# A fused attention and spectral-mix kernel: two more units of the output stage take the last mode's rows by a table, unit 3 goes in halves, and one weight tile is issued ahead of a gate

## The chip, the cores and the metric

One core of a Trainium2 chip runs the whole kernel. The metric is device microseconds (us) of one execution; a kernel's time is the median of its runs. The span is the part of one profiled execution from its first to its last recorded instruction; the profiled execution also has a time of its own, which is a little longer than its span.

## The reference

Two parts are computed one after the other; shapes are batch 8, 8 heads, 576 tokens, head size 64.

```python
# attention: window of 128 keys, a linear distance penalty per head
scores = q @ k.T / sqrt(64); scores = where(0 <= rel < 128, scores - slope[h] * |rel|, -1e9)
x = softmax(scores) @ v                 # [8, 576, 512] after joining the heads
# spectral mix: 64 complex modes, each with a 512 x 512 weight w_r + i w_i (float32, 1 MB each)
X = rfft(x, axis=tokens)[:, :64]
Y = X @ (w_r + i w_i)                   # mode by mode
u = x + irfft(Y)                        # the other modes are zero
out = u + relu(u @ w_ch)                # w_ch is 512 x 512
```

The weights of the 64 modes are 128 tiles of 1 MB in float32, which the DMA casts to bfloat16 (512 KB) as it loads them.

## The kernel before, in words

The order on each engine is the program's own order (a manual schedule); waits are semaphores set by a tile library that tracks which part of which tile is read and written.

**Attention** runs over 16 units (a batch and a group of four heads) in the order of the list `STAGE`. The q, k and v of a unit are loaded by the SP queue (lines L211, L215, L222) into the raw buffers, two units deep. Between the stages GpSimd (POOL) issues weight tiles (`load_w`, L462), one per stage into the pool `early`. A one-element copy on POOL (L556), called the gate, ties each to the progress of attention. From stage 12 on weight tiles also go into the raw buffers of q, k and v that are no longer needed (`spare`). At stage n - 3 = 13 a second gate copy (L559) reads four elements of the last unit's raw v, so POOL stops there until those v rows have landed.

**The weight stream.** Groups of four modes are multiplied with the spectra XC on TensorE (PE, line L897) as their tiles come in; POOL loads the next tiles into buffers as they come free (L462, L481, L489). Meanwhile PE projects the units' tokens (`project`, `augment`) so that little is left for the end. The results per mode are kept, one row per mode and part, as Z (for u) and as ZW (already multiplied with w_ch); a product with a slice of the inverse table FT turns rows into tokens (`spread`, L654).

**The tail.** There are 18 output units: a pair of batches and 128 tokens each (units 0 to 3 belong to batches 0 and 1, units 4 to 7 to batches 2 and 3, unit 8 holds the last 64 tokens of batches 0 to 3, and so on). For a unit, `activate(j)` brings up `mm` = u @ w_ch on PE (`begin`: restore XW; `channels`: the products with the rows of ZW) and ScalarE (ACT) takes relu to `r` (L800). `finish(j)` brings up `yy` = u on PE (L757, L654) and VectorE (DVE) adds both (L825), and SP writes the result out (L830, L837). The order on PE is activate(1), finish(1), activate(2), finish(2), activate(3), and then activate(j) ahead of finish(j - 1). The two psum slots of each kind are used in turn.

The last modes arrive too late for this: rows 0 to 6 of the last eight come from `late_end`, rows 6 and 7 (mode 63) from the very last product. `patch` copies them row by row into Z and ZW by small DMAs, on SP or POOL. Units 0 to 3 don't wait for all of it: unit 0 takes the late rows by a product with the table `FM` (`last_rows`, L781), and units 1 to 3 (the tuple `FIRST`) use only 62 rows of ZW and take mode 63's by a product of `ywp` (the un-summed w_ch rows of mode 63, `zp` copied by DVE and ACT, L980 and L981) with the table `FM3`. FM and FM3 lie in a part of YT that is no longer used and are filled by small SP DMAs in `last_tables`. For unit 0 the end is written out by hand: product of y, first half (L971), four products into zp, product with FM (L979), two with FM3 (L982), the sum `zs` of ywp (L984), product of y, second half (L986), after which ACT copies it to r (L992) and copies zs to the rows of yw (L995) that POOL then patches into ZW (L996). `HALVES` names the units whose relu, add and write go in two halves of 256 KB rather than one of 512 KB.

Of the kernel before, what the change touches and what calls it, by code (L numbers as in the profile page):

```python
# [11 lines left out]
BF16 = mybir.dt.bfloat16  # L12
# [390 lines left out]
def kernel(  # L403
# [49 lines left out]
    def load_w(n, pool, chosen=None):  # L453

        for i in ([i for i in todo_w if i not in again][:n] if chosen is None else chosen):
            todo_w.remove(i)
            src = (moe_w_r, moe_w_i)[i % 2][i // 2].rearrange("(p a) e -> p a e", a=4)
            homes[i] = pool
            t = spare.pop(0) if pool is None else pool.tile([P, 4, DM], BF16, tag="w", name="w")
            for part in ((slice(0, 4),) if i < 2 * NM - 1  # L460
                         else (slice(0, 2), slice(2, 3), slice(3, 4))):
                nc.gpsimd.dma_start(out=t[:, part], in_=src[:, part])  # L462
            wq[i] = [t[:, a] for a in range(4)]
# [27 lines left out]
    with ExitStack() as actx:  # L491
        at = _Attention(tc, actx, q, k, v, (ident, F, FT), x, XC, raw)
        n = len(at.units)
        for w, u in (("q", 0), ("k", 0), ("q", 1), ("k", 1), ("v", 0), ("v", 1)):
            at.load(w, u)
        done = set()

        def run(name, arg, u):
            if 0 <= u < n and (name, arg, u) not in done:
                done.add((name, arg, u))  # L500
                getattr(at, name)(u, arg)

        make_identity(nc, ident)
        pool = _Scratch(x[:, B - 2 :].rearrange("p b t c -> p (b t c)").bitcast(FP32))
        wt = at.ps.tile([P, P], FP32, tag="av", bufs=1, name="warm")
        for _ in range(24):
            nc.tensor.matmul(wt, lhsT=ident, rhs=ident, start=True, stop=True)
        table = _forward_table(nc, pool, F, S)
        next(table)
        nc.vector.memset(norm, 2.0 / S)  # L510
        nc.vector.memset(norm[:32], 1.0 / S)
        for t in at.qkT:
            nc.vector.memset(t[:, 1, :, S:], 0.0)
        at.distances(pool)
        at.fixtures(0)
        load_w(1, early)
        next(table, None)
        at.fixtures(1)
        nc.gpsimd.memset(XC[:, 4 * NC * NM :], 0.0)
        run("cast", "q", 0)  # L520
        run("transpose", "q", 0)
        run("cast", "k", 0)
        run("transpose", "k", 0)
        run("evacuate", "q", 0)
        for h in (1, 3):
            at.decay(h)
        run("evacuate", "k", 0)
        run("score", 1, 0)
        for h in (0, 2, 1, 3):
            at.offset(h)  # L530
        run("cast", "q", 1)
        run("transpose", "q", 1)
        run("evacuate", "q", 1)
        run("score", 0, 0)
        run("exp", 1, 0)
        for h in (0, 2):
            at.decay(h)
        run("exp", 0, 0)
        run("cast", "k", 1)
        run("cast", "v", 0)  # L540
        side = {0: [(at.offset, 4), (at.offset, 6), (at.decay, 5), (at.offset, 5), (at.decay, 7),
                    (at.offset, 7), (at.decay, 4), (at.decay, 6)]}
        lags = [lag for _, _, lag in STAGE]
        for stage in range(min(lags), n + max(lags)):
            for name, arg, lag in STAGE:
                run(name, arg, stage - lag)
                if name in ("transpose", "exp") and side.get(stage):
                    for _ in range(1 + (name == "transpose")):
                        fn, h = side[stage].pop(0)
                        fn(h)  # L550
            if stage == 3:
                at.inverse_table()
            if stage in AHEAD:
                if stage:
                    b, g = at.units[stage - 1]
                    nc.gpsimd.tensor_copy(gate[:1, :1], x[:1, b, 0, 256 * g : 256 * g + 1])  # L556
                load_w(AHEAD[stage], early)
            if stage == n - 3:
                nc.gpsimd.tensor_copy(gate[:1, :4], raw["v"][:1, (n - 1) % 2, 1, :, 0])  # L559
            if stage in LATER:  # L560
                load_w(LATER[stage], None)

    with ExitStack() as mctx:
        fix = mctx.enter_context(tc.tile_pool(name="fix", bufs=1))
# [12 lines left out]
        def late_end(acc):  # L577

            rows = slice(0, 96)
            yq = pool.tile([P, DM], BF16, tag="yq", bufs=3)  # L580
            nc.vector.tensor_scalar_mul(yq[rows], acc[rows], 2.0 / S)
            patch(nc.gpsimd, range(2, B), yq, Z, 0, 6)
            yield
            tr = lps.tile([P, 4, P], BF16, tag="tr", name="tr")
            for et in range(4):
                nc.tensor.transpose(tr[:, et, rows], yq[rows, et * P : (et + 1) * P],
                                    ident[rows, rows])
            yT = pool.tile([P, 2, 4, P], BF16, tag="xT", name="xT")[:, 0]
            nc.vector.tensor_copy(yT[:, :, rows], tr[:, :, rows])
            heads[LAST] = yq, yT  # L590
            yield
            zl = heads["z"].tile([P, DM], FP32, tag="z0", name="zl")
            for et in range(4):
                nc.tensor.matmul(zl[rows], lhsT=yT[:, et, rows], rhs=wch[:, et],
                                 start=(et == 0), stop=(et == 3))
            nc.scalar.copy(yw[rows], zl[rows])
            patch(nc.sync, (0, 1), yw, ZW, 0, 6)

        def quad_end(acc, g):

# [37 lines left out]
        def patch(queue, bs, rows, dst, lo=0, hi=8):  # L638

            for b in bs:  # L640
                r = 64 * (b % 2) + 8 * (LAST % 8)
                queue.dma_start(out=dst[r + lo : r + hi, b // 2, 1],
                                in_=rows.rearrange("(k v) e -> k v e", v=16)[lo:hi, b])
# [84 lines left out]
            nc.scalar.copy(src[:, 0], ys[0])  # L728
            nc.vector.tensor_copy(src[:, 1], ys[1])  # L729

        HALVES, FIRST = (0, 1, 2, len(units) - 1), (1, 2, 3)
        mms, yys, rs = {}, {}, {}

        def pair(tag, slot=0):
# [52 lines left out]
        def activate(j):  # L787

            if j in FIRST:
                if j not in mms:  # L790
                    begin(j)
                channels(j, 62)
                last_rows(mms[j][0], j, ywp, FM3)
            else:
                begin(j)
                channels(j)
            mm, slot = mms.pop(j)
            r = rs[j] = heads["out"].tile([P, 2, DM], FP32, tag="r", name="r")
            for c in parts(j):
                nc.scalar.activation(r[:, c], mm[:, c], AF.Relu)  # L800
            idle.append(slot)
# [40 lines left out]

        sides = (slice(0, DM // 2), slice(DM // 2, DM))
        quads, side, recycle = [], [], list(again)
        ZW = Z = XW = FC = pairs = wch = w2 = None
        dead = YT[:, 0].rearrange("p e b m r -> p (e b m r)")
        FM = dead[:, : 2 * P].rearrange("p (b s) -> p b s", b=2)
        FM3 = dead[:, 2 * P : 10 * P].rearrange("p (b s) -> p b s", b=2)
# [2 lines left out]
        def last_tables():  # L851

            nc.gpsimd.memset(dead[:, : 10 * P], 0.0)
            for et in range(4):
                rows = slice(32 * et, 32 * et + 32)
                nc.gpsimd.tensor_copy(fold[rows], ident[rows, rows])
            by_row = [t.rearrange("(k v) b s -> k v b s", v=16) for t in (FM, FM3)]
            for b in range(2):
                top = 64 * b + 2 * HM - 8
                nc.sync.dma_start(out=by_row[0][:, b, b], in_=FT[top : top + 8, b, :P])  # L860
                for et in range(4):
                    nc.sync.dma_start(out=by_row[1][2 * et : 2 * et + 2, b, b],
                                      in_=FT[top + 6 : top + 8, b, : 4 * P])

        yw = F[:, : DM // (2 * NM)].rearrange("p a b -> p (a b)")
        ywp = XC[:, :DM]
        K1 = spot[again[-1]]
        for g in range(NM // 4):
# [5 lines left out]
            for i in range(8):  # L874
# [35 lines left out]
                if k == K1:  # L910
# [10 lines left out]
                    ZW = right.tile([P, B // 2, 2, DM], BF16, name="ZW")  # L921
                    Z = right.tile([P, B // 2, 2, DM], BF16, name="Z")
                    XW = right.tile([P, len(units), 2, DM], BF16, name="XW")
                    FC = right.tile([P, P], BF16, name="FC")
                    pairs = right.tile([P, P], BF16, name="pairs")
                    nc.gpsimd.memset(FC, 0.0)
# [46 lines left out]
        for i, c in enumerate(sides):  # L973
            for et in range(4):
# [4 lines left out]
        last_rows(mms[0][0], 0, yw, FM, 96)  # L979
        nc.vector.tensor_copy(ywp[:, sides[0]], zp[0])  # L980
        nc.scalar.copy(ywp[:, sides[1]], zp[1])  # L981
        last_rows(mms[0][0], 0, ywp, FM3)  # L982
        zs = zps.tile([P, DM], FP32, tag="z0", name="zs")
        nc.tensor.matmul(zs[96:], lhsT=fold, rhs=ywp, start=True, stop=True,  # L984
                         tile_position=(0, 96))
        last_rows(yy, 0, yq, FM, ns=(1,))  # L986
        lctx.close()
        heads["mm"].append(mctx.enter_context(
            tc.tile_pool(name="mps", bufs=1, side="right", space=PSUM, reuse_waits="tile")))
# [3 lines left out]
        free.append(slot)  # L993
        rs[0] = r
        nc.scalar.copy(yw[96:], zs[96:])  # L995
        patch(nc.gpsimd, (2, 3), yw, ZW)  # L996
        patch(nc.gpsimd, (6, 7), yq, Z, 6, 8)
        patch(nc.gpsimd, (0, 1), yw, ZW, 6, 8)
        patch(nc.gpsimd, range(4, B), yw, ZW)
# [46 lines left out]
```

## Time and profile before

| | |
|---|---|
| median of 3 runs | 442.16 us (441.75 to 444.46) |
| the profiled execution's time | 443.43 us |
| its span | 441.7 us |
| PE busy | 322.6 us (73%) |
| DVE, ACT, POOL busy | 185.3, 162.9, 89.2 us |
| bytes moved by DMA | 105.55 MB, mean 239 GB/s |
| attention ends, stream and projection go on | near 140 us |
| last weight products begin | 403 us |
| first output write issued | 409.6 us |
| last add of DVE ends | 433.4 us |

How to read it: a line is the line of the kernel's program, `out<-in` names the tiles; "issue" is time in which an engine waited for nothing that the profile shows; PEld is the load of the stationary operand; q0 is the queue of POOL's DMAs and q1 that of SP's. The DMA share is the mean over 16 engines and can pass 1, since packets of one engine overlap. Bytes are counted as written, so a weight tile counts 512 KB.

### The profile page before, as it was taken

The numbers are of one execution on the slowest core, as the hardware profiler recorded it, in microseconds if no ns is written. First come the engines' busy times: TensorE is split into PE (matmuls) and PEld (weight loads), VectorE is DVE, ScalarE is ACT, GpSimd is POOL, SyncE is SP. The second block draws the span as 40 slices with busy tenths as digits, with TensorE's granted clock in tenths as the row PEclk, the third lists the DMA queues.
The fourth block names the chain that finished last, engine by engine and source line by source line (L and its number), as shares of the span: only waits on it lengthen the run. The fifth ranks groups of instructions, "written<-read, shape, count | busy, mean of one in ns | idle before, by whom it ended". The sixth has DMA issues, their size and how long they took to land.

```text
span 441.7 us, 8353 instructions
## 1 busy us (share of the span) xinstructions
PE 322.6 (73%) x3524; PEld 179.0 (41%) x3524; DVE 185.3 (42%) x333; ACT 162.9 (37%) x211; POOL 89.2 (20%) x168
## 2 busy tenths in 40 slices
PE   5679899898796634543442487999885999999891
PEld 4357676675664411111111133444442444344340
DVE  7799898787873301010000021331222222222692
ACT  6849899698780000000000011232221322212780
POOL 8711010101134001321111110111131020113500
PEclk9979999899998965555555579999999899999997
DMA  8999999999999999999999999999999999996598
GB/s 286 316 319 306 275 318 296 308 300 275 242 190 213 214 214 214 214 214 214 215 212 215 214 214 214 214 215 215 214 213 215 214 214 215 215 213 123 189 355 323
DMA packets 52573, 105.55 MB, mean 239 GB/s; under 512 B 4136, under 2 KB 23480, under 8 KB 52536
## 3 DMA queue, kind: packets, MB, share of 16 engines
q0 software_dynamic: 19024, 67.22, 76.2%
q1 hardware_dynamic: 33512, 37.81, 26.2%
q8 instruction: 27, 0.44, 0.4%
q14 instruction: 10, 0.08, 0.1%
HBM read 162.53 MB, written 9.44 MB: 389 GB/s over the span
## 4 chain that ended last, share of the span: by engine, by line
DMA 68%; PE 12%; DVE 9%; issue 5%; ACT 3%; POOL 1%; SPq 0%; DVEq 0%; POOLq 0%; ACTq 0%
DMA w<-in_moe_w_r_dram 43%; DMA w<-in_moe_w_i_dram 15%; DMA qr<-in_q_dram 5%; PE av L334 3%; DMA vr<-in_v_dram 2%; DMA kr<-in_k_dram 2%; PE xt L371 2%; PE tp L253 1%; DVE att L308 1%; DVE x L350 1%; DVE o L825 1%; DVE vb L236 1%; DVE q L241 1%; PE acc L897 1%; DMA ZW<-F 1%
## 5 line engine op out<-in xcount | busy, mean ns | idle before, releaser
L897 PE MATMUL acc<-w,XC 128*32 128x512 bf16 (+1 forms) x464 | 81.3, 482 | 65.5 <-DMA w<-in_moe_w_r_dram 32.2
L897 PEld LDWEIGHTS <-XC 128*32 128x32 bf16 x516 | 38.9, 148 | 107.3 <-issue 80.2
L297 ACT ACTIVATE att<-sc 128x1024 bf16<-128x1024 f32 x64 | 64.0, 1032 | 11.1 <-PE sc L287 11.1
L630 ACT CAST ZW<-zw 128x512 bf16<-128x512 f32 x8 | 4.7, 585 | 140.6 <-PE zw L628 140.6
L334 PE MATMUL av<-vb,att 128*128 128x132 bf16 (+1 forms) x576 | 38.9, 219 | 13.6 <-DVE x L350 8.1
L334 PEld LDWEIGHTS <-att 128*128 128x128 bf16 x704 | 37.1, 99 | 19.0 <-DVE x L350 12.3
L697 PE MATMUL my<-wch,xT 128*64 128x512 bf16 x288 | 35.6, 388 | 10.0 <-DVE x L729 4.3
L602 DVE TENSOR_SCALAR yq<-acc 128x512 bf16<-128x512 f32 x14 | 9.6, 686 | 78.1 <-PE acc L897 78.1
L706 ACT CAST XW<-my 128x512 bf16<-128x512 f32 x36 | 19.3, 589 | 56.3 <-PE my L654 56.3
L678 DVE COPY xT<-tr 128x1024 bf16<-128x1024 bf16 x18 | 12.4, 691 | 54.7 <-PE tr L676 54.7
L259 ACT COPY qkT<-tp 128x1152 bf16<-128x1152 bf16 x30 | 33.5, 1115 | 2.4 <-PE tp L253 1.8
L481 POOL DMA_DIRECT2D w<-in_moe_w_r_dram x22 | 15.6, 709 | 76.9 <-PE acc L897 51.8
L481 POOL DMA_DIRECT2D w<-in_moe_w_i_dram x23 | 16.1, 700 | 72.8 <-PE acc L897 45.5
L697 PEld LDWEIGHTS <-xT 128*64 128x64 bf16 x288 | 17.4, 110 | 26.2 <-issue 14.1
L350 DVE TENSOR_TENSOR x<-av,rec 128x640 bf16<-128x640 f32 x32 | 26.4, 824 | 1.1
L287 PE MATMUL sc<-qkT 64*64 64x256 bf16 (+2 forms) x640 | 25.3, 265 | 2.1 <-ACT qkT L259 1.2
L236 DVE CAST vb<-vr 64x1024 bf16<-64x1024 f32 x32 | 22.7, 708 | 0.4 <-DMA vr<-in_v_dram 0.2
L556 POOL COPY gate<-x 1x1 bf16<-1x1 bf16 x13 | 5.5, 421 | 85.3 <-DVE x L350 85.3
L287 PEld LDWEIGHTS <-qkT 64*64 64x64 bf16 x640 | 14.6, 109 | 19.0 <-issue 16.0
L728 ACT CAST x<-my 128x512 bf16<-128x512 f32 x18 | 10.5, 585 | 30.3 <-PE my L654 30.3
L274 PE MATMUL sc<-bias,ident 128*128 128x512 bf16 x64 | 20.4, 402 | 1.4 <-ACT att L297 1.4
L825 DVE TENSOR_TENSOR o<-yy,r 128x1024 f32<-128x1024 f32 (+1 forms) x20 | 20.0, 1056 | 3.2 <-PE yy L654 2.3
(145 smaller groups left out, 439.3 us busy)
## 6 DMA issues: line engine op xcount, KB each, us to landing
w<-in_moe_w_i_dram POOLq DMA_DIRECT2D x23, 1024.0 KB, 36.3
w<-in_moe_w_r_dram POOLq DMA_DIRECT2D x22, 1024.0 KB, 36.3
qr<-in_q_dram SPq DMA_DIRECT2D x16, 576.0 KB
kr<-in_k_dram SPq DMA_DIRECT2D x16, 576.0 KB
vr<-in_v_dram SPq DMA_DIRECT2D x64, 128.0 KB
w<-in_moe_w_r_dram POOLq DMA_DIRECT2D x16, 512.0 KB, 14.3
w<-in_moe_w_i_dram POOLq DMA_DIRECT2D x13, 512.0 KB, 24.0
out_dram<-o SPq DMA_DIRECT2D x13, 512.0 KB
```

The source lines that it names most:

```text
L236: nc.vector.tensor_copy(self.vb[u % 2][row, :, :, :, W * half : W * half + D], src[row, :2])
L259: (self.nc.vector.tensor_copy if u < 2 and w == "q" else self.nc.scalar.copy)(dst.rearrange("q h (p j) -> q h p j", j=TPP), tp.rearrange(" ...
L274: nc.tensor.matmul(sc[:, e], lhsT=self.ident, rhs=self.bias[:, hv].rearrange("p j n -> p (j n)"), start=True, stop=False, skip_group_check ...
L287: nc.tensor.matmul(sc[64 * half : 64 * half + 64, e, j * 256 + c0 : j * 256 + c0 + n], lhsT=qkT[row, 1, h, k0 + j : k0 + P : 2], rhs=qkT[r ...
L297: self.nc.scalar.activation(self.att[u % 2][:, kt * 8 * P : (kt + 1) * 8 * P], sc.rearrange("p e n -> p (e n)"), AF.Exp, scale=1.0 / math. ...
L334: nc.tensor.matmul(bank[:, qt * W : qt * W + rhs[j].shape[1]], lhsT=att[:, o : o + P], rhs=rhs[j], start=(n == 0 and j == 0), stop=(n == l ...
L350: nc.vector.tensor_tensor(out=self.x[:, b, :, cs].rearrange("p t (h d) -> p h t d", h=2), in0=tiles[:, :, :, :D], in1=rec.unsqueeze(-1).br ...
L481: nc.gpsimd.dma_start(out=t.rearrange("p s a e -> p s (a e)"), in_=w[kinds.pop()][m : m + 2].rearrange("m (p a) e -> p m (a e)", a=4))
L697: nc.tensor.matmul(mm[ROWS[half]], lhsT=lhsT, rhs=wch[:, dt], start=(dt == 0), stop=False, skip_group_check=True,)
L706: nc.scalar.copy(XW[:, j, n], mms[n])
L825: nc.vector.tensor_tensor(out=o[:, c], in0=yy[:, c], in1=r[:, c], op=ALU.add)
L897: nc.tensor.matmul(to[32 * (m % 4) : 32 * (m % 4) + 32], lhsT=XC[:, c0 : c0 + 31 * NM + 1 : NM], rhs=wq[t][a][:, c], start=(ri == 0 and a ...
```

## The change

Four edits. In the attention part, stage 13 issues one of its two weight tiles before the copy that waits for v, and the other after it. Units 4 and 5 join `FIRST`: they use 62 rows of ZW and take mode 63's rows by a product with a new table, `FM2`, which covers batches 2 and 3 and 256 tokens, lies in the pool `late`, and is cleared by a memset on POOL and filled by eight more small SP DMAs. The patch of batches 2 and 3 in ZW is cut in two: rows 0 to 6 go in `late_end`, rows 6 and 7 where all eight went before. Unit 0's second y product moves ahead of the products with FM3 and of zs. Unit 3 joins `HALVES`.

```diff
-            if stage == n - 3:
-                nc.gpsimd.tensor_copy(gate[:1, :4], raw["v"][:1, (n - 1) % 2, 1, :, 0])
             if stage in LATER:
-                load_w(LATER[stage], None)
+                if stage == n - 3:
+                    load_w(1, None)
+                    nc.gpsimd.tensor_copy(gate[:1, :4], raw["v"][:1, (n - 1) % 2, 1, :, 0])
+                load_w(LATER[stage] - (stage == n - 3), None)
...
             patch(nc.sync, (0, 1), yw, ZW, 0, 6)
+            patch(nc.gpsimd, (2, 3), yw, ZW, 0, 6)
...
-        HALVES, FIRST = (0, 1, 2, len(units) - 1), (1, 2, 3)
+        HALVES, FIRST = (0, 1, 2, 3, len(units) - 1), (1, 2, 3, 4, 5)
...
-                last_rows(mms[j][0], j, ywp, FM3)
+                last_rows(mms[j][0], j, ywp, FM2 if units[j][0] else FM3)
...
             nc.gpsimd.memset(dead[:, : 10 * P], 0.0)
+            nc.gpsimd.memset(FM2, 0.0)
...
-            by_row = [t.rearrange("(k v) b s -> k v b s", v=16) for t in (FM, FM3)]
+            by_row = [t.rearrange("(k v) b s -> k v b s", v=16) for t in (FM, FM3, FM2)]
...
                     nc.sync.dma_start(out=by_row[1][2 * et : 2 * et + 2, b, b],
                                       in_=FT[top + 6 : top + 8, b, : 4 * P])
+                    nc.sync.dma_start(out=by_row[2][2 * et : 2 * et + 2, 2 + b, b],
+                                      in_=FT[top + 6 : top + 8, b, : 2 * P])
...
+                    FM2 = right.tile([P, 2, 2 * P], BF16, name="FM2")
...
+        last_rows(yy, 0, yq, FM, ns=(1,))
         last_rows(mms[0][0], 0, ywp, FM3)
         zs = zps.tile([P, DM], FP32, tag="z0", name="zs")
         nc.tensor.matmul(zs[96:], lhsT=fold, rhs=ywp, start=True, stop=True,
                          tile_position=(0, 96))
-        last_rows(yy, 0, yq, FM, ns=(1,))
...
-        patch(nc.gpsimd, (2, 3), yw, ZW)
+        patch(nc.gpsimd, (2, 3), yw, ZW, 6, 8)
```

More of the change, by code (lines that the diff above doesn't have):

```diff
@@ L844 @@
         quads, side, recycle = [], [], list(again)
-        ZW = Z = XW = FC = pairs = wch = w2 = None
+        ZW = Z = XW = FM2 = FC = pairs = wch = w2 = None
         dead = YT[:, 0].rearrange("p e b m r -> p (e b m r)")
```

## The prediction, as put on record before the change was run

> **What bounds the kernel now.** I read the chain of work that ended last first, because it says which resource ends each stage:
>
> ```profile
> DMA 68%; PE 12%; DVE 9%; issue 5%; ACT 3%; POOL 1%; SPq 0%; DVEq 0%; POOLq 0%; ACTq 0%
> ```
>
> Two thirds of the span is waiting for transfers, nearly all of it for the weights of the 64 modes. So the question for each edit is what it does to the transfers. The windows view (columns: stretch, length, busy us of PE, PEld, DVE, ACT, POOL, then granted PE clock, DMA share, GB/s) shows where the DMA engines are not full:
>
> ```profile
> 118.00:123.50 5.50, 5.11 (x94) 3.69 (x91) 4.04 (x9) 5.20 (x6) 0.96 (x3) 1.00 1.11 257
> 123.50:126.00 2.50, 2.50 (x52) 1.92 (x43) 1.82 (x3) 2.02 (x4) 2.13 (x4) 1.00 0.65 101
> 128.00:403.00 275.00, 190.71 (x1451) 87.80 (x1448) 56.76 (x122) 38.73 (x69) 46.80 (x78) 0.80 1.06 214
> 410.00:416.00 6.00, 4.73 (x56) 1.75 (x60) 3.27 (x5) 4.01 (x8) 4.80 (x10) 1.00 0.66 231
> 416.00:419.00 3.00, 2.85 (x51) 1.42 (x42) 2.69 (x3) 2.97 (x4) 0.48 (x1) 1.00 0.45 159
> 419.00:426.00 7.00, 6.86 (x92) 2.94 (x88) 6.79 (x7) 5.76 (x7) 0.00 (x0) 1.00 1.03 377
> 426.00:427.00 1.00, 0.95 (x16) 0.43 (x16) 1.00 (x2) 0.90 (x1) 0.00 (x0) 1.00 0.33 119
> 427.00:440.00 13.00, 5.29 (x56) 2.04 (x55) 6.92 (x7) 4.17 (x5) 0.00 (x0) 0.89 1.02 379
> ```
>
> The weight stream runs full (share 1.06, 214 GB/s) for 275 us, so its end is its start plus its bytes. It starts with a hole at 123.5 to 126. From 419 the output writes are full too (377 and 379 GB/s). Before that there are holes at 410 to 419, and a short one at 426. Only filling a hole can move the end. The 18 units write 9.44 MB, 24.9 us at 379 GB/s; the writes lie between 410.45 and 440.2, 29.75 us, so 4.85 us of the tail is holes.
>
> The hole of the head, in the timeline of POOL:
>
> ```profile
> 118.25 0.53 POOL L462 DMA_DIRECT2D w<-in_moe_w_i_dram  x1
> 123.31 0.18 POOL L559 CAST gate<-vr 1x4 bf16<-1x4 f32 x1 [4.53 <-DMA vr<-in_v_dram]
> 123.82 0.54 POOL L462 DMA_DIRECT2D qr<-in_moe_w_r_dram  x1 [0.33 <-issue]
> ```
>
> POOL holds its next weight tiles until the last unit's v rows are in (4.53 us of waiting). Then it issues, and the data starts about 1.7 us later. The hole of the tail, in the timeline and the waits:
>
> ```profile
> 413.51 0.41 PE L757 MATMUL mm<-XW,ident 64*64 64x512 bf16 x4
> 415.19 0.58 PE L654 MATMUL mm<-ZW,FT 64*64 64x512 bf16 x4 [1.27 <-DMA ZW<-F]
> 416.31 5.89 DVE L825 TENSOR_TENSOR o<-yy,r 128x1024 f32<-128x1024 f32 x5 [2.30 <-PE yy L654]
> ```
>
> Unit 4's mm waits 1.27 us for the patched ZW rows, and because finish(3) stands behind activate(4) on PE, unit 3's output waits too: DVE sits 2.30 us, and the next write is issued at 417.56.
>
> **The change, part by part.**
>
> *One tile ahead of the gate.* One 512 KB tile (2.45 us at 214 GB/s) is issued right behind that of 118.25, near 118.8; its buffer, the raw q of an odd unit, was last cast at 110.87 to 111.7, so POOL does not wait. The DMA view for 112 to 130 shows that the software queue serves its tiles one after the other:
>
> ```profile
> w<-in_moe_w_i_dram POOLq DMA_DIRECT2D x1, 512.0 KB, 7.2
> qr<-in_moe_w_r_dram POOLq DMA_DIRECT2D x1, 512.0 KB, 5.0
> kr<-in_moe_w_r_dram POOLq DMA_DIRECT2D x1, 512.0 KB, 7.0
> kr<-in_moe_w_i_dram POOLq DMA_DIRECT2D x1, 512.0 KB, 9.9
> vr<-in_moe_w_i_dram POOLq DMA_DIRECT2D x1, 512.0 KB, 11.8
> ```
>
> The tile of 118.25 lands at 125.45, and the four behind the gate, issued 0.53 us apart, land 2 to 3.5 us apart. So the added tile starts where its forerunner thins out, at about 123.5, and its 2.45 us lie in the hole. Worth: by the share 2.5 x (1.06 - 0.65) / 1.06 = 0.97 us, by the bytes 2.5 x (214 - 101) / 214 = 1.32 us. I take the middle, 1.15. Later tiles are issued when they were, and the stream, full for 275 us, ends 1.15 us sooner. What it may delay is the tail of v (121 small packets of queue q1 between 123.5 and 126) and so the end of attention; that is covered by about 17 tiles queued at 137.5, over 40 us of transfers. Lower bound 0: the hole is only moved. Upper bound 1.32.
>
> The Trainium skill, DMA: Bandwidth & Descriptors, section Queues, rings and completion order, says that each DMA engine takes turns between the queues that have work. The trace shows turns that are far from even: at 122.5 to 123.5 q0 has 100% and q1 5%. By that rule the tile would push v back as soon as it is queued; its result is the first rival below.
>
> *Tables for units 4 and 5.* Removed: the wait of 1.27 us. Added: two 128x512 products per unit. The nearest rows are units 1 to 3, which do this already: unit 2's mm begins at 410.91 and unit 3's at 412.44, 1.53 us per unit, against 1.13 us of units without (416.88 to 418.01). So +0.4 us of PE twice. *Preparing the table*: a POOL memset of 512 columns beside one of 1280 that takes 1.18 us, so 0.47 us, into an idle of 2.83 us ahead of the next load at 333.68; eight small SP issues at 2.52 / 4 = 0.63 us, 5 us on a queue that is idle until 405.8. Both nothing; if the cover were gone, 0.5 us of a POOL that issues tens of us ahead. *The patch in two parts*: two more POOL issues of 0.55 us at 405.9 to 407.0; behind them stand the four Z patches that began at 407.21, so these slip by 0 to 0.3 us, and their first reader comes after 415. The second part is needed by unit 6 near 416.5 and is issued near 410.2; the 8 KB patch issued at 411.49 landed by 415.19.
>
> *Unit 0's y product first.* PE waits for the casts until 408.14; the product of 0.21 to 0.39 us moves into that gap. ACT then copies r near 408.5 instead of 409.46, DVE's second half goes at 409.6 instead of 410.08, and ACT is free for unit 1 sooner. Worth about 0.25 us for units 1 to 3, bounds 0 and 0.45; a loss of 0.2 if the first half's products slip by one product.
>
> *Unit 3 in halves.* ACT 1.08 us for 1.02 and DVE 1.29 for 1.21, one more SP issue of 0.37; the first half is out 0.53 us before a whole would be.
>
> *Sum of the tail.* PE begins unit 4 at 413.25 (413.50 - 0.25). From a unit's mm to the end of the next yy took 1.70 us at unit 2 (410.91 to 412.61), so unit 3's yy ends at 414.95, before at 416.2. DVE halves are out at 415.65 and 416.3; from issue to first packet takes 0.9 us (417.56 to 418.46), so unit 3 writes from 416.55, where unit 2's writes end (416.7). Unit 4: yy at 414.95 + 1.53 = 416.5, DVE 1.21, issue, 0.9: writes from 418.6. Before, full writing began at 418.46 with unit 3's own 512 KB (1.38 us), so unit 4 began at 419.85. Gain 1.25 us. From there DVE delivers a unit each 1.13 us and the writes take 1.38, so the writes stay full and the table's 0.8 us of PE is hidden. Bounds: 0.15 if an SP issue stalls as that of unit 1 did (1.24 us, the longest L830 issue, for 0.37); 1.9 if the hole at 426 also closes.
>
> Together 1.15 + 1.25 = 2.4 us: span 441.7 to 439.3, its time 443.43 to 441.0. The profiled run is 1.27 us above the median 442.16, so I forecast a median of 439.8.
>
> **The rivals.**
>
> *The added tile delays v: no gain in the head.* For: v's packets and the tile share the engines, and the gate opens only with v; then POOL's next tiles start later by what the tile took, and the hole only moves. Against: the one-by-one landings above. Then 1.25 us alone: 440.9.
>
> *The tail's gain is swallowed.* A write issue that stalls, or PE late again at unit 6's patched rows. For: stalls of the size exist at units 1 and 8. Against: unit 6's patch has over 2 us of slack. Then the head alone plus 0.15: 440.9.
>
> *Everything closes.* All 4.85 us of holes of the tail less the first packets' start, with 1.32 in the head, would be up to 6 us: 436.2. For: the first halves come 0.45 us closer. Against: units 1 and 2 are spaced by ACT and DVE halves, which the change leaves alone.
>
> *Slower: PE drops to half clock in the tail.* Place: units 3 to 17. In the stream the clock was 0.50 at 200 to 240 and L897 products took 630 ns, and 392 at clock 1.00 in 384 to 403: 1.6 times. A unit of 1.13 us would take 1.8, above the 1.38 us of its write, and this is the point from which it decides: 14 x 0.45 = 6.3 us, less the 2.4: 446.1. For: the clock does drop in this kernel. Against: it was 1.00 from 384 to 437, through the very wait that goes away, and the change adds work to PE. The Trainium skill, TensorE: Matmul & The Clock Gate, section What's actually happening, gives about 3.4 us of idling as what drops the clock; the trace agrees so far that 1.27 us did not.
>
> **How the numbers follow.** Forecast 0.53, own range 438.9 to 441.2 (sum with its bounds); no gain in the head 0.12; tail swallowed 0.12; everything closes 0.16; slower 0.07. Median: 439.8. The range 437.6 to 442.6 reaches past both half-gains, to runs as much scattered as the three shown, and half way to the everything case. A measurement tells about 1% (4.4 us) from no change: faster than 437.7 is the everything case and the far edge of the forecast, 0.18; slower than 446.6 is the clock case, counted whole because a drop from 413 on costs more than one from 416, 0.07; the rest, 0.75, is within 1%.
>
> **What would show it.** Right: the window 123.5 to 126 at a DMA share over 0.95; PE with no wait for ZW at unit 4; the last weight products near 402; the window 416 to 419 at a share over 0.75. Wrong: the gate's wait over 6 us, a DMA share below 0.8 anywhere in 120 to 128, an idle of DVE over 1.5 us ahead of unit 3, or output writes below 1.0 after 420 other than at unit 8.

## The result, and the profile after

| | before | changed | ratio, 95% interval |
|---|---|---|---|
| median of 22 runs each | 444.14 us (440.77 to 446.45) | 446.60 us (443.59 to 449.28) | 1.0064 (1.0038 to 1.0089) |
| profiled execution: time, span | 443.43, 441.7 us | 446.8, 444.8 us | |

The change makes the kernel slower by 0.64%, 2.8 us; the forecast was 2.4 us faster. (Here the unchanged kernel itself ran 2.0 us above the median that the forecast started from. The ratios leave out runs over 1.5% above the fastest of their kernel, which below are three of the twelve runs of e1 and one of e4; counted whole, e1's mean is 442.9 us beside 443.1 for the kernel before, nearly no gain.)

The loss is not where any of the four edits was meant to act. It arises between 330 and 348 us, where the table of units 4 and 5 is filled. In `last_tables` the eight new loads (L867 after) stand between the ten that fill FM and FM3. FM and FM3 lie in the dead half of the tile YT, so the profile names those ten `YT<-FT`. The other half of YT is in use: DVE's copy of a group's results (`COPY YT<-tr`, L612 before, L614 after) waits until those ten loads are in. The loads write `YT[:, 0]` and the copy writes `YT[:, 1]`, so no data make it wait; e6 below shows that sharing the tile does. Timeline lines of SP, DVE and PE, before (start, us, engine, line, what it does, and in brackets the idle time ahead of it and what ended it):

```profile
334.12 2.41 SPq L862 DMA_DIRECT2D YT<-FT  x4
341.04 0.50 DVE L612 COPY YT<-tr 128x128 bf16<-128x128 bf16 x2 [7.36 <-DMA YT<-FT]
342.18 1.92 PE L697 MATMUL my<-wch,xT 128*64 128x512 bf16 x8 [4.30 <-DVE x L729]
```

And the changed kernel:

```profile
341.77 0.56 SPq L865 DMA_DIRECT2D YT<-FT  x1
346.83 0.50 DVE L614 COPY YT<-tr 128x128 bf16<-128x128 bf16 x2 [11.76 <-DMA YT<-FT]
347.97 1.92 PE L699 MATMUL my<-wch,xT 128*64 128x512 bf16 x8 [8.69 <-DVE x L731]
```

Read from the top: the last `YT<-FT` issue ends at 336.53 before (334.12 + 2.41) and at 342.33 after, because an `FM<-FT` issue now stands between nearly all of them (the first of the ten went at 329.99 and at 331.39, so they take 6.54 us and 10.94). DVE's copy comes 4.5 us after that end in both. Its idle time grows from 7.36 to 11.76, by 4.40 us; behind the copy in DVE's order stands the cast `x`, and PE's next projection waits for that cast: 4.30 becomes 8.69, by 4.39 us. The chain of waits of the changed kernel between 325 and 410 us carries it (start, us, what):

```profile
336.17 4.97 DMA YT<-FT
341.77 4.99 DMA YT<-FT
347.33 0.60 DVE x L731
```

The two pieces of transfer are there, 5.0 us each, and the longer pieces of the chain from 347 on are PE, with some ACT and DVE, and no transfer: PE is the bound until the last weight product. That is seen where PE waits for weight tiles, in the waits of PE between 330 and 405 us (engine, tile, line, releaser: us in all, times, longest). Before:

```profile
PE pa L897 <- DMA w<-in_moe_w_i_dram: 0.7, 3, 0.3
...
PE pa L897 <- DMA w<-in_moe_w_r_dram: 0.5, 2, 0.3
...
PE acc L897 <- DMA w<-in_moe_w_r_dram: 0.3, 1, 0.3
```

Changed:

```profile
PE acc L902 <- DMA w<-in_moe_w_i_dram: 0.6, 1, 0.6
```

Before, PE has caught up by 390.80 us and waits a quarter of a microsecond for each of the last six tiles; these three lines, 1.45 us by the timeline, are its whole reserve. In the changed kernel the one wait left lies at 337.21, ahead of the stall, and none follows. The last weight products but one, before and then changed:

```profile
403.08 1.03 PE L897 MATMUL acc<-w,XC 128*32 128x256 bf16 x8 [0.30 <-DMA w<-in_moe_w_r_dram]
```

```profile
407.29 1.09 PE L902 MATMUL acc<-w,XC 128*32 128x256 bf16 x8
```

The first waits for its weights, the second doesn't: by the DMA view the last piece of the weights landed at 405.6 us before (issued at 391.04, 14.6 us to landing) and at 405.8 after (391.32 and 14.5), but PE is busy with older work. It starts 4.2 us later, and so does the last group, at 409.30 for 405.04. The account: DVE's copy is 5.79 us later (346.83 for 341.04), 4.40 by the loads and 1.40 because this execution was that much later already when the loads began; less the reserve of 1.45 that leaves 4.3, beside 4.2 measured. From the start of the last group to the end of the span took 36.7 us before (441.7 - 405.04) and 35.5 after (444.8 - 409.30): the tail was 1.2 shorter. Together 4.2 - 1.2 is the 3.1 us between the spans, within rounding.

The windows of the tail, moved by 4.3 us so that they answer to the four from 410 to 427 of the kernel before (columns as there):

```profile
414.30:420.30 6.00, 6.00 (x69) 1.88 (x72) 3.72 (x7) 4.37 (x8) 5.15 (x10) 1.00 0.67 231
420.30:423.30 3.00, 2.90 (x43) 1.33 (x36) 2.76 (x4) 2.86 (x3) 0.00 (x0) 1.00 0.80 296
423.30:430.30 7.00, 6.86 (x94) 3.07 (x93) 6.79 (x6) 5.93 (x6) 0.00 (x0) 1.00 0.92 337
430.30:431.30 1.00, 0.93 (x20) 0.53 (x16) 1.00 (x2) 0.89 (x2) 0.00 (x0) 1.00 1.03 381
```

The share of the second is 0.80 where it was 0.45: the hole ahead of unit 3's output is mostly filled. That of the third is 0.92 for 1.03 and of the last 1.03 for 0.33, because unit 8's hole now comes earlier. Share times length adds up to 13.9 us of transfers, before 12.9: 1.0 us more of the writes is done by the same point.

### The profile page after: what moved, and what is told of

Read it like the earlier page. It is cut to its first block, busy times and chain, and to the rows that moved or that the text cites. A ratio compares the mean times of both kernels' runs of the same rounds, so it can differ in the third digit from the quotient of the medians.

```text
span 444.8 us, 8381 instructions
## 1 busy us (share of the span) xinstructions
PE 324.5 (73%) x3528; PEld 180.0 (40%) x3528; DVE 185.4 (42%) x334; ACT 163.1 (37%) x212; POOL 90.9 (20%) x171
## 4 chain that ended last, share of the span: by engine, by line
DMA 52%; PE 27%; DVE 9%; ACT 3%; issue 3%; SPq 2%; POOL 1%; DVEq 0%; POOLq 0%; ACTq 0%
DMA w<-in_moe_w_r_dram 29%; DMA w<-in_moe_w_i_dram 8%; DMA vr<-in_v_dram 6%; PE my L699 5%; DMA qr<-in_q_dram 5%; PE acc L902 4%; PE my L656 2%; PE av L334 2%; DMA YT<-FT 2%; DMA kr<-in_k_dram 2%; PE pa L902 1%; PE xt L371 1%; DVE vb L236 1%; PE tp L253 1%; PE yy L759 1%
## 5 line engine op out<-in xcount | busy, mean ns | idle before, releaser
L902 PE MATMUL acc<-w,XC 128*32 128x512 bf16 (+1 forms) x464 | 80.2, 473 | 64.9 <-DMA w<-in_moe_w_i_dram 31.9
L297 ACT ACTIVATE att<-sc 128x1024 bf16<-128x1024 f32 x64 | 64.1, 1032 | 13.9 <-PE sc L287 13.9
L699 PE MATMUL my<-wch,xT 128*64 128x512 bf16 x288 | 35.6, 388 | 14.4 <-DVE x L731 8.7
L287 PEld LDWEIGHTS <-qkT 64*64 64x64 bf16 x640 | 14.6, 109 | 19.8 <-issue 16.7
```

What stands on the lines that cost most here:

```text
L287: nc.tensor.matmul(sc[64 * half : 64 * half + 64, e, j * 256 + c0 : j * 256 + c0 + n], lhsT=qkT[row, 1, h, k0 + j : k0 + P : 2], rhs=qkT[r ...
L297: self.nc.scalar.activation(self.att[u % 2][:, kt * 8 * P : (kt + 1) * 8 * P], sc.rearrange("p e n -> p (e n)"), AF.Exp, scale=1.0 / math. ...
L699: nc.tensor.matmul(mm[ROWS[half]], lhsT=lhsT, rhs=wch[:, dt], start=(dt == 0), stop=False, skip_group_check=True,)
L902: nc.tensor.matmul(to[32 * (m % 4) : 32 * (m % 4) + 32], lhsT=XC[:, c0 : c0 + 31 * NM + 1 : NM], rhs=wq[t][a][:, c], start=(ri == 0 and a ...
```

## The experiments

Each ratio is against the kernel before, run between on the same chip.

**e1_fill_last, e2_fill_only, e3_fill_last_no_head, e4_head_only** separate the filling of the table, the head and the tail. e1 is the changed kernel with the eight loads in a loop behind the ten:

```diff
-                    nc.sync.dma_start(out=by_row[2][2 * et : 2 * et + 2, 2 + b, b],
-                                      in_=FT[top + 6 : top + 8, b, : 2 * P])
+            for b in range(2):
+                top = 64 * b + 2 * HM - 8
+                for et in range(4):
+                    nc.sync.dma_start(out=by_row[2][2 * et : 2 * et + 2, 2 + b, b],
+                                      in_=FT[top + 6 : top + 8, b, : 2 * P])
```

> The changed kernel with one move: the eight small loads that fill FM2 are issued after all ten that fill FM and FM3, instead of between them. Theory (fill): the interleaved loads put the last YT<-FT load back by about 5 us, DVE's copy into YT behind the multiply of the group waits for it (11.8 us instead of 7.4), PE stands and ends the stream late. Then this kernel's DVE wait is back near 7.4 us, the first half of the last weight products begins near 402 to 403 instead of 407.3, and the time is 4 to 5 us below the changed kernel's, about 442 and 0.3 to 0.6% below before. Rival (head): the tile ahead of the gate delays attention; then the time stays near 446 and only the DVE wait shortens. Rival (tail): the extra products and halves cost; also near 446.

Measured: 444.14 us, ratio 0.9973 (0.9935 to 1.0010). Its twelve runs fall into two groups, five from 438.6 to 440.9 and seven from 444.1 to 446.7, with nothing between. DVE's wait is back to 7.10 us in its profile:

```profile
343.66 0.50 DVE L614 COPY YT<-tr 128x128 bf16<-128x128 bf16 x2 [7.10 <-DMA FM<-FT]
```

The view names a load of FM2 as what ended it, but the issues of those eight end only at 344.38, and the copy comes 4.25 us behind the last `YT<-FT` issue. e7, the same kernel once more, names `YT<-FT`.

e2 is the kernel before with the memset and the eight interleaved loads alone; nothing reads the table:

```diff
+            nc.gpsimd.memset(FM2, 0.0)
...
+                    nc.sync.dma_start(out=by_row[2][2 * et : 2 * et + 2, 2 + b, b],
+                                      in_=FT[top + 6 : top + 8, b, : 2 * P])
```

> The kernel before with nothing but the preparation of FM2 (tile, memset, eight small loads between those of FM and FM3); the table is never read. Theory (fill): DVE waits 11 to 12 us for YT<-FT, the last weight products begin 3 to 4.5 us later, and the time is 3 to 4.5 us (0.7 to 1.0%) above before. Rivals (head, tail): same time as before within 0.2%.

Measured: 447.43 us, ratio 1.0086 (1.0053 to 1.0119), 3.8 us slower. Its timeline of DVE, and its waits:

```profile
346.73 0.50 DVE L612 COPY YT<-tr 128x128 bf16<-128x128 bf16 x2 [11.63 <-DMA YT<-FT]
```

```profile
PE my L697 <- DVE x L729: 8.6, 1, 8.6
```

Both waits, 11.63 and 8.6 us, are nearly those of the changed kernel (11.76 and 8.69). Loads that nobody reads cost 3.8 us, the whole change 2.8, with intervals that overlap, so the loss does not come from what the table is used for. That it comes from their place in the SP queue is shown by e7 below.

e3 is e1 with the gate of before, which leaves the edits of the tail; e4 is before with the edit of the head alone.

```diff
-                if stage == n - 3:
-                    load_w(1, None)
-                    nc.gpsimd.tensor_copy(gate[:1, :4], raw["v"][:1, (n - 1) % 2, 1, :, 0])
-                load_w(LATER[stage] - (stage == n - 3), None)
+                load_w(LATER[stage], None)
```

(This is e3, which has the copy ahead of the `if` again, as before; e4 is the reverse.)

> As the first of these runs (FM2 filled last), with the gate of before (no tile ahead of it). What it differs by from the first run is the worth of the head edit. Theory (prediction's head term): 1.0 to 1.3 us slower than the first run, with a hole in the DMA share behind the gate. Rival (head hurts): 1 us or more faster than the first run. The tail's own gain against before is then 1.0 to 1.3 us (0.25%).

> The kernel before with the head edit alone. Theory (prediction's head term): 1.0 to 1.3 us below before (0.25%), the DMA share in the 2.5 us around the gate's end near 1.06 instead of 0.65. If PE is what ends the stream, because the DVE wait of 7.4 us leaves it no slack, then less: 0 to 0.5 us. Rival (head hurts): 1 us or more above before.

Measured: e3 442.37 us, 0.9998 (0.9968 to 1.0028); e4 444.47 us, 1.0001 (0.9963 to 1.0038). Neither shows a gain here. e4's profile shows two things that bear on the head's. Its POOL, then its queues between 120 and 126 us (packets, MB, share), then a window:

```profile
117.84 0.54 POOL L462 DMA_DIRECT2D qr<-in_moe_w_r_dram  x1
127.67 0.70 POOL L561 CAST gate<-vr 1x4 bf16<-1x4 f32 x1 [9.30 <-DMA vr<-in_v_dram]
```

```profile
q0 software_dynamic: 280, 1.03, 85.4%
q1 hardware_dynamic: 367, 0.17, 12.2%
```

```profile
126.00:128.00 2.00, 1.91 (x41) 1.71 (x41) 0.71 (x2) 1.88 (x3) 0.33 (x1) 1.00 0.09 21
```

The first: the added tile is issued at 117.84, and its last packets end at 126.98, just before the gate opens at 127.67. The last v rows trickle in beside it (12.2% of the engines' time); then the engines do nearly nothing for four microseconds (a share of 0.09, and 0.03 in the two that follow). But this is not the edit's doing alone: in e3, with the gate of before, POOL waits 8.01 us at the same place. The DMA share between 120 and 140 us measures the hole (full is 1.07): 1.02 before and 1.08 after, but 0.84, 0.83, 0.83 and 0.81 in e1 to e4, or 20 x (1.07 - 0.83) / 1.07 = 4.5 us.

The second is what the expectation of e4 named. Behind DVE's copy no weight product waits for its weights, and the last but one, which waits in before and in e7, doesn't either:

```profile
405.49 1.03 PE L898 MATMUL acc<-w,XC 128*32 128x256 bf16 x8
```

In that execution PE's work, not the transfers, ended the stream, so weights that come sooner at its end gain nothing. Whether weights that come sooner ahead of the stop do (PE waits 0.6 us for a tile there) isn't shown.

**e5_no_v_gate, e6_own_tile, e7_fill_last_again, e8_no_head_again.** e5 is e1 without the copy that waits for v, so that its `if` holds only `load_w(LATER[stage], None)`. e6 is the changed kernel with the gate of before, the loads interleaved, but FM, FM3 and `fold` in a tile of their own:

```diff
-        dead = YT[:, 0].rearrange("p e b m r -> p (e b m r)")
...
+                    dead = right.tile([P, 10 * P + 32], BF16, name="tables")
+                    FM = dead[:, : 2 * P].rearrange("p (b s) -> p b s", b=2)
```

e7 and e8 are the kernels of e1 and e3 again, unedited.

> The changed kernel with FM2 filled last and without the copy that waits for the last unit's v rows, so that no weight tile is held back by it. Open question: the hole in the DMA share behind that copy measured 0 to 4.8 us from one profile to the next, with the head edit (0.04, 4.28, 4.75) and without (1.08, 4.43, 4.57). Theory (hole): the copy itself makes the hole; without it the hole is under 0.5 us in the profile, the slower group of runs is gone, and the time is 2 to 4 us below the kernel with the head edit. Rival (v starves): v then trickles in beside the weights, attention ends 3 us or more later, the later tiles that wait for attention leave a hole elsewhere, and the time is the same or worse.

> The changed kernel with the gate of before, and with FM, FM3 and fold in a tile of their own instead of in the unused half of YT; the eight loads of FM2 stand between the others as in the change. Theory (fill): only what waits for the loads made them cost; DVE's copy into YT has nothing to wait for now, PE has no stop of 4 to 9 us near 338, and the time equals that with FM2 filled last (tail gain only, 0.2 to 0.3% below before). It is not faster than that, since PE waits for weights at the end again. Rival (the loads themselves cost, by DMA time or SP): 3 us or more slower, as with the loads between on the YT halves.

> FM2 filled last, with the head edit, a second time beside the next one. If the edit makes the long hole behind the gate more frequent, over half of the runs lie in the upper group (above 443.5 us), and the lower group is 1 to 2 us below the lower runs without the edit. If it only fills the hole, the whole spread lies about 1 us below that of the next kernel.

> FM2 filled last, with the gate of before, a second time. The tail's gain of 1.1 us is there in each run; the median is 0.2 to 0.3% below before. About a third of the runs in the upper group, as for the kernel before.

| | us | ratio |
|---|---|---|
| e5 | 440.72 (439.13 to 442.50) | 0.9935 (0.9912 to 0.9958) |
| e6 | 442.00 (440.86 to 444.29) | 0.9966 (0.9946 to 0.9987) |
| e7 | 442.28 (439.66 to 444.90) | 0.9971 (0.9937 to 1.0006) |
| e8 | 442.86 (440.55 to 445.29) | 0.9979 (0.9948 to 1.0009) |

e7, with the loads last, in the timelines of DVE and PE:

```profile
338.30 0.50 DVE L614 COPY YT<-tr 128x128 bf16<-128x128 bf16 x2 [7.29 <-DMA YT<-FT]
400.35 1.03 PE L905 MATMUL acc<-w,XC 128*32 128x256 bf16 x8 [0.27 <-DMA w<-in_moe_w_r_dram]
```

The wait is that of before (7.29 for 7.36) and PE waits for its last weights again. e7 and the changed kernel differ in the order of the eight loads only: 0.9971 against 1.0064 is 0.93%, or 4.1 us, with an interval of some 1.9 us either way (the two intervals added in squares). e7's reserve by its waits is 0.5 us, that of before 1.45, so 4.4 us of delay should cost an estimated 3.0 to 3.9; e2's 3.8 and this 4.1 agree within their intervals.

e6 takes away the shared tile. DVE's copy no longer waits for a load, and PE gains reserve in the stream (timelines of DVE and PE):

```profile
334.26 0.50 DVE L613 COPY YT<-tr 128x128 bf16<-128x128 bf16 x2 [0.49 <-PE tr L607]
385.60 1.14 PE L898 MATMUL acc<-w,XC 128*32 128x512 bf16 x8 [2.40 <-DMA w<-in_moe_w_i_dram]
```

PE's waits for weights from 375 us on add up to 4.6 us (1.45 before), though the eight loads are interleaved as in the changed kernel. It also shows that the 7.36 us wait of before cost that kernel little: e6 is 0.13% below e8, within the intervals.

e5 has one group of times, without e1's upper one. Its window:

```profile
120.00:140.00 20.00, 15.88 (x290) 12.47 (x287) 13.55 (x26) 11.78 (x15) 7.02 (x12) 1.00 1.08 222
```

At a share of 1.08 there is no hole: without the gate the stream starts full. (POOL still waits for v once, 2.56 us ahead of 123.31, for the buffer that held v; four tiles are queued by then.) e5 is 2.9 us faster than before (1.9 to 3.9), with the edits of the tail in it. Beside e8, the same kernel with the gate of before, it is 2.0 us faster, with an interval of 1.7 either way.

**e9_own_tile_no_gate, e10_halves_only, e11_y_first_only, e12_tables_only.** e9 joins what helped: the changed kernel with the tables in their own tile and no copy waiting for v. e10 to e12 are the kernel before with one edit of the tail each: 3 in `HALVES`; unit 0's second y product first; the tables for units 4 and 5 (loads last) with the patch in two parts.

> The version that the runs point to: the changed kernel with the three tables in a tile of their own and without the copy that waits for the last unit's v rows. Expected like the kernel without that copy, 0.5 to 0.7% below before, with no stop of DVE near 340 and no hole behind 118. If the stop near 340 did cost something (rival: PE's slack was negative before), another 0.2% or more below.

> The kernel before with unit 3 in halves alone. Read from the profile: the time from the start of the last eight weight products to the end of the span (before 36.6 us, changed 35.5). Expected about 36.6 to 36.2: the wait for the ZW rows is still there, so only the first half's 0.5 us can come forward.

> The kernel before with unit 0's second y product ahead of the table products alone. Same reading: 36.6 to 36.3 us; ACT's copy into r about 0.9 us earlier, the patch of ZW that unit 4 waits for about 0.5 us earlier and with it unit 3's write.

> The kernel before with the tables for units 4 and 5 alone, FM2 filled last. Same reading: 36.6 less 0.5 to 0.9 us; no wait for ZW at unit 4, 1.5 us of PE per unit for units 4 and 5.

Measured: e9 440.37 us (439.51 to 441.23), ratio 0.9923 (0.9895 to 0.9951): 3.4 us faster than before, the best of all, though e5's interval overlaps with it. The other three ran once: 444.18, 445.55 and 443.13 us beside 443.69 for before; single times say nothing at this size. From the last group of products to the end they took 36.05, 36.1 and 35.6 us (before 36.7, all edits 35.5). Of the three only the tables (e12) take PE's wait for ZW away, and DVE's longest wait for `yy` is down to 1.3 us there; halves leave the wait for ZW at 1.0 and y first at 1.2 (before 1.27). How the 1.2 us divides is settled no further: in e10 and e11 the hole at unit 8, 0.7 us before, happened to be nearly absent, which explains most of their 0.6.

## Why the prediction was wrong, point by point

*The step that failed is "Preparing the table", the sentence "eight small SP issues at 2.52 / 4 = 0.63 us, 5 us on a queue that is idle until 405.8. Both nothing".* The 5 us was right: the last `YT<-FT` issue ends 4.4 us later relative to the first (10.94 us behind its start after, 6.54 before). The cover was wrong. The queue was idle, but its loads had a reader: DVE, and PE behind it. "If the cover were gone, 0.5 us of a POOL" named the memset and left the loads out. The row that spoke against it was in the trace of before: DVE's 7.36 us, ended by `DMA YT<-FT`. The prediction read what was free on SP, and not who waits for what SP loads. None of the rivals held it; the slower one, a half clock in the tail, did not come (granted clock 1.00 from 410 to 426 and 0.98 to 440); nor did the swallowed tail, nor everything closing.

*"The stream, full for 275 us, ends 1.15 us sooner", and with it the end.* This took PE as covered by the transfers. The weights did come in nearly as before, 405.8 for 405.6, though attention in that execution ran 2.0 us later already ahead of the edit (the gate of stage 13 at 119.77 for 117.80). PE's reserve was 1.45 us, and in other executions less: 0.5 in e7, none in e4. That the chain of waits names transfers had hidden that PE's work is nearly as long: a bound that leads by 1.45 us in 275 is no cover for another engine's delay.

*The head, 1.15 us.* In the changed kernel's profile the mechanism is there: the window from 123.5 to 126 us holds a share of 1.11 where it was 0.65, and POOL's wait is what it was (a line of POOL's timeline, and the window):

```profile
125.87 0.18 POOL L561 CAST gate<-vr 1x4 bf16<-1x4 f32 x1 [4.59 <-DMA vr<-in_v_dram]
```

```profile
123.50:126.00 2.50, 2.21 (x40) 1.60 (x38) 2.35 (x5) 2.02 (x4) 0.13 (x1) 1.00 1.11 230
```

But the term was sized from one execution, and the hole that it fills isn't a constant: in the twelve profiles with the gate the wait runs from 4.5 to 8.1 us without the edit and from 4.6 to 10.4 with it. In times the edit is worth -0.7 us with an interval of 1.5 either way (the mean of e1 and e7 less that of e3 and e8): neither 1.15 nor nothing is excluded. Whether it makes the long wait more frequent, as two groups in e1 and e7 might suggest, stays open. The rival "the added tile delays v" fails in the short waits (4.59 us with the tile, 4.53 to 4.66 without) and fits the long ones: 9.3 and 10.4 us with it (e4, e1), 8.0 to 8.1 without (e2, e3, e12), and the same hole between 120 and 140 us, so that there the hole only moved. These are a few single executions, so it isn't shown. In e4's packet records single packets of v come 0.34 us apart from 124.58 to 126.96, each where a weight packet of 0.32 us ends. As soon as the last weight packet has ended, at 126.98, the remaining packets of v follow each other every 0.02 to 0.03 us. By that rhythm one engine (the records don't name it) gave v and a weight tile turns, and the last tile queued was the added one. The Trainium skill, DMA: Bandwidth & Descriptors, section Queues, rings and completion order, has an engine change queues packet by packet. The turns of one v packet to one weight packet in e4 agree with that, and so do its 367 packets of v beside 280 of weights, at 12.2% of the time, as its packets are small. The prediction had called the turns uneven by time (100% and 5% at 122.5 to 123.5); in packets that stretch has 52 and 33. The changed kernel's profile, with 1899 packets of q1 beside 180 of q0 in the same six microseconds, doesn't look like equal turns.

*The tail, 1.25 us.* Right in mechanism, and near in size: the profile is 1.2 shorter. PE has no wait for ZW at unit 4, a unit with the table takes 1.55 us (unit 4's mm begins at 417.49, the next at 419.04) where 1.53 was expected, and DVE's idle ahead of unit 3 is 1.34 us where it was 2.30:

```profile
417.49 0.41 PE L759 MATMUL mm<-XW,ident 64*64 64x512 bf16 x4
417.73 0.39 PE L656 MATMUL mm<-ZW,FT 62*64 62x512 bf16 x4
418.05 0.60 PE L783 MATMUL mm<-XC,FM 128*128 128x512 bf16 x2
419.33 1.29 DVE L827 TENSOR_TENSOR o<-yy,r 128x512 f32<-128x512 f32 x2 [1.34 <-PE yy L656]
```

Not all of the 1.2 is the edits': e2 and e4 have the tail of before too, and from the last group of products to the end e4 takes 36.7 us and e2 35.7, with hardly a hole at unit 8. The eight profiles with all edits of the tail take 35.1 to 35.5, so the gain read this way is 0.2 to 1.6. In times e3 and e8, which have the tail alone, average -0.5 us, with an interval of about 1.0 either way: 1.25 is within it, and so is nothing. The extra patch issues cost nothing that shows.

*The signs listed.* Three came out as written for "right": the head's window, no wait for ZW, and, moved with the tail, a share of 0.80 where 416 to 419 was to pass 0.75. The remaining one, "the last weight products near 402", read 407 to 409, and it was the one that held the answer. Of the signs listed for "wrong", none came in the changed kernel's profile, read with the tail moved as before; the gate's wait over 6 us came in e1 and e4. With the table's loads out of the way the change measured -1.2 us (0.9973 and 0.9971) where -2.4 was forecast: half in size, and both intervals reach past no change.

*The own range.* Its slow end, 441.2, doesn't come out of the bounds given: with 0 for the head and 0.15 for the tail the sum is 442.0. Both lie below the 446.6 measured, which the table's loads account for. "Nearly all of it for the weights" reads the chain too high: weights are 58 of the 68% (43 and 15).

## What to carry to other kernels

A load on an idle queue isn't free when loads behind it have a waiting reader: find the readers of everything on that queue in the waits, and put new loads behind those whose readers are due first. A small table that borrows the dead part of a tile in use borrows that tile's waits too. Where transfers bound a stage, also read how long the compute engine waits at the stage's end: that wait is all the delay that it can take.

## What the runs showed that I had not expected

A load of 2 KB on the SP queue, issued beside the full weight stream, was in 5.0 us after its issue began (4.97 and 4.99 in the chain), with little scatter: in the twelve profiles that have the tables in YT, DVE's copy followed the end of the last such issue by 4.25 to 4.57 us.

With a transfer that POOL waits for while the weights run, one program can have two groups of times, some 5 us apart (e1: near 440 and 445 us). Without that gate the spread of times is 3.4 us in e5 and 1.7 in e9; but e6, with the gate, spreads no more than e5, so that the gate alone makes the groups is not shown. The length of the hole varies by more than 4 us between executions of the same kind of kernel, so one profile can't size what an edit at that place is worth.
